# A decode block's last weight, w2: 192 of its rows laid three to a partition on 64 partitions

## The chip, the cores and the metric

The kernel runs on one core of one Trainium2 chip. The metric is device microseconds of one execution, from the first to the last thing that the core does; the median of the runs is given. Before the change it is 665.03 us, the median of three runs (664.89 to 667.58).

The core has five engines that run beside each other: PE (TensorE, matrix products, with its weight loads shown apart as PEld), DVE (VectorE), ACT (ScalarE), POOL (GpSimd) and SP (SyncE), which here only issues transfers. Sixteen DMA engines move the data.

## What is computed

One decoding step of an attention block with cache, followed by a dense block with the mish activation; four sequences, one new token each.

```python
def _A_ref(x, k_cache, v_cache, wq, wo):
    q = (x @ wq).reshape(B, Sq, H, Dh) transposed to (B, H, Sq, Dh)
    scores = jnp.einsum("bhqd,bhkd->bhqk", q, k_cache) * (Dh ** -0.5)
    p = _softmax(scores, axis=-1)
    o = jnp.einsum("bhqk,bhkd->bhqd", p, v_cache)
    return o (heads joined) @ wo

def _B_ref(x, w1, b1, w2):
    h = jnp.einsum("bsd,df->bsf", x, w1) + b1
    sp = jnp.log1p(jnp.exp(-jnp.abs(h))) + jnp.where(h > 0, h, 0)
    act = h * jnp.tanh(sp)
    return jnp.einsum("bsf,fd->bsd", act, w2)

h = x + _A_ref(_layernorm(x), k_cache, v_cache, wq, wo)
h2 = h + _B_ref(_layernorm(h), w1, b1, w2)
```

B = 4, Sq = 1, D = 640, 32 heads of 128, 4096 cached positions, F = 1728; everything is bf16. The two caches are 268 MB of the 283 MB that the kernel reads. w2 is 1728 x 640, 2.21 MB.

## The kernel before

**An order written out by hand.** A small class, `Program`, takes every operation with its engine, the things it reads and writes, and a function that emits it. `add` (L41) notes what an operation has to wait for: writers of what it reads, readers and writers of what it overwrites, and whatever is named in `after`. Each engine then runs its operations strictly in the order in which they were added, and waits on semaphores. Operations that carry a `sem` are transfers; each completed transfer adds 16 to its semaphore. SP's and POOL's operations are emitted first, as straight lists (L218); DVE, ACT and PE have a part ahead of a loop, the loop's body, and a part behind it.

**The stream.** The 16 units (8 heads of one sequence each) need one K tile and one V tile each, 128 partitions of 65,536 bytes. They go through three buffers, `slot0` to `slot2`. K is multiplied by the query on DVE (L639), summed over the head's dimensions by products with an identity on PE (L651), reduced (L626), and turned into weights of the softmax (L688 to L736); V is multiplied on PE (L761). SP issues all these transfers on one queue. As soon as a slot has been read for the last time, the weights of the end go into it: wo and w1 into slot `i1` (`wend`), w2 into slot `i2` (`wend2`), and the working tiles of the end behind w2 (`scratch`, L918).

**The order of SP's last transfers** (L884 to L914): wo in two pieces (L885), w1 in three (L886), then w2. The first w2 transfer waits for `last_pv`, the PE products that read V of the last unit but one from slot `i2`.

**How w2's rows lie.** F = 1728 is 13 blocks of 128 rows and 64 rows more. The first 12 blocks are laid in pairs: a partition takes two neighbouring rows, 2560 bytes, in one packet. Block 12 is single, 1280 bytes a partition. The pieces are `W2P = (0, 6, 10, 12, C2)`, four transfers. The 64 rows left are a transfer of their own, ahead of these: they go to every second partition (`w2r_sb[1::2, :]`, L903), over a memset to zero by POOL (L897) that they wait for.

**How the activations follow that.** `f_rows(c)` (L533) says which 128 columns of w1 block `c` takes, so that the activation comes out on the partition where its row of w2 lies: every second column for a block of a pair, 128 neighbouring ones for block 12. The block that holds the 64 left over, number `C2` = 13, takes the last 128 columns, half of which block 12 has too. `FC` = 14 blocks, so b1 is turned in 14 columns (L570), each of the five passes over w1 (`h1_pass`, L1051) makes 14 products, and the mish chain works on 56 columns (L1083 to L1113). To bring the last 64 activations to every second partition, with zeros between, a 0/1 matrix `apart` is built by POOL (L935, L938), and one PE product (L1154) and an ACT copy (L1158) move block 13's activations into `act_r`.

**The last products.** `residual` puts h into the output bank. `w2_products` (L1135) makes four products for each block, one for each quarter of the output's 640 columns. The order on PE is: residual, the turning product, blocks 0 to 5, the 64 rows left over, blocks 6 to 9, blocks 10 and 11, block 12; each piece waits for its own transfer. Then DVE and ACT gather the four quarters (L1166) and SP stores them (L1175).

Of the kernel before, what the change touches and what calls it, by code (L numbers as in the profile page):

```python
# [8 lines left out]
BF16 = mybir.dt.bfloat16  # L9
ACT = mybir.ActivationFunctionType  # L10
# [224 lines left out]
def kernel(  # L235
# [13 lines left out]
    nc = tc.nc  # L249

    B, Sq, D = A_x.shape
    _, H, Sk, Dh = A_k_cache.shape
    F = B_w1.shape[1]
    N = B * Sq
    DC = D // 128
# [20 lines left out]
    CT = 128 // (G * RQ)  # L276
    VQ = 2

    C2 = F // 128
    FM = C2 * 128  # L280
    FREM = F - FM
    FC = C2 + 1
    W2P = (0, 6, 10, 12, C2)
    W1P = (0, 2, 4, DC)
    OT4 = 4
    DT = D // OT4
    OVER = 128 - FREM


    pad = -int(nc.sbuf_base) % 512  # L290
# [11 lines left out]
    slot = [slots.tile([128, SLOT], BF16, name=f"slot{i}") for i in range(NS)]  # L302
    banks = [ps.tile([128, 512], FP32, name=f"bank{i}") for i in range(8)]
    s_bank, tr_bank, qq_bank, o_bank, oT_bank = banks[0:4], *banks[4:8]
    S_BANK, TR, QQ, OB, OT = [("bank", i) for i in range(4)], *[("bank", i) for i in range(4, 8)]

    def const(shape, dt, name):
        return consts.tile(shape, dt, name=name)

    ident = const([128, 128], BF16, "ident")  # L310
# [4 lines left out]
    nscale = const([1, 128], FP32, "nscale")  # L315
    b1T = const([128, FC], FP32, "b1T")

# [28 lines left out]
    P = Program(nc, tc, 1, NU - 1, NS)  # L346
# [4 lines left out]
    def cells(i, lo=0, hi=SLOT):  # L351

        return [("slot", i, p, k) for p in range(lo // PART, -(-hi // PART)) for k in range(NQ)]
# [5 lines left out]
    def load_kv(what, rows, u, i, parts=1):  # L359
        w = SLOT // parts  # L360
        for k in range(parts):
# [24 lines left out]
        w=cells(0, 0, o0),  # L386
        sem="wq",
# [4 lines left out]
        w=["b1"],  # L392
        sem="b1",
# [9 lines left out]
            out=ident[:, :],  # L403
            in_=ident[:, :],
# [7 lines left out]
        w=["ident"],  # L412
# [5 lines left out]
        w=["ident_f"],  # L418
# [12 lines left out]
    def bn_stats():  # L431
        for s in range(2):
# [8 lines left out]
        w=["mv"],  # L441
# [4 lines left out]
            out=ln_std[:, :], in_=ln_mv[:, 1:2], func=ACT.Sqrt, bias=eps_t[0:N, :], scale=1.0  # L446
        ),
        r=["mv", "eps"],
        w=["std"],
# [5 lines left out]
        w=["rstd1"],  # L455
# [4 lines left out]
            out=ln1_bf,  # L460
# [7 lines left out]
        w=["ln1"],  # L468
# [19 lines left out]
    for src, dst, r, w in (  # L488
# [8 lines left out]
            w=[w],  # L497
# [3 lines left out]
    def identity_sums(dst, pattern, name, **kw):  # L501
# [13 lines left out]
            out=own[:, :], in0=own1[:, :], scalar1=-1.0, scalar2=1e30, op0=ALU.add, op1=ALU.mult  # L515
        ),
        r=["own1"],
        w=["own"],
# [8 lines left out]
        w=["dq_m"],  # L527
# [3 lines left out]
    )  # L531

    def f_rows(c):  # L533
        if c < C2 - C2 % 2:
            f0 = c // 2 * 256 + c % 2
            return slice(f0, f0 + 255, 2)
        f0 = c * 128 if c < C2 else F - 128
        return slice(f0, f0 + 128)


    qT_ps = qq_bank[:, 0 : N * H].rearrange("p (b h) -> p b h", b=N)
# [1 line left out]
    def q_all():  # L543
        for h in range(H):
# [15 lines left out]
            out=qT[:, 0 : NU * G].rearrange("p (o b g) -> p b o g", o=NO, b=N),  # L560
            in_=qT_ps[:, :, :].rearrange("p b (o g) -> p b o g", o=NO),
        ),
        r=[QQ],
        w=["qT"],
    )
    b_ps = oT_bank[:, 0:FC]

    def b1_turned():
        for c in range(FC):
            ins = nc.tensor.matmul(  # L570
                b_ps[:, c : c + 1],
                lhsT=b1_row[:, f_rows(c)],
                rhs=ident[0:1, 0:1],
                start=True,
                stop=True,
            )
        return ins
# [256 lines left out]
    def slot_of(u):  # L834
        return 1 if u == 0 else 2 * u % NS

    for u in range(NU):
# [10 lines left out]
        if u >= 1:  # L848
            last_pv = pv(u - 1, 0 if u == 1 else slot_of(u - 1), u)
# [7 lines left out]
    i1, i2, i3 = slot_of(NU - 1), slot_of(NU - 2), slot_of(NU - 3)  # L857
    wend, wend2 = slot[i1], slot[i2]
# [3 lines left out]
    wo_view = A_wo.rearrange("(w p j) n -> p w j n", w=NW, j=J)  # L862
    nw2 = FC * D
    w2_sb = wend2[:, 0 : C2 * D].rearrange("p (k n) -> p k n", k=C2)
    w2r_sb = wend2[:, C2 * D : nw2]
    C2E = C2 - C2 % 2
    w2_view = B_w2[0 : C2E * 128, :].rearrange("(m p k) n -> p m (k n)", p=128, k=2)

    def load(out_ap, in_ap, i, lo, hi, name, sem=None):


        ops = {}
        for cell in cells(i, lo, hi):
            for d in P.readers.get(cell, {}).values():
                ops[d.nth] = d
        P.add(
            "SP",
            lambda: nc.sync.dma_start(out=out_ap, in_=in_ap),  # L878
            w=[name],
            sem=sem or "_".join(map(str, name)),  # L880
            after=ops.values(),
        )
# [3 lines left out]
    for k0, k1 in zip(W1P, W1P[1:]):  # L886
# [5 lines left out]
            nwo + k1 * F,  # L892
            ("w1", k0),
        )
    P.add(
        "POOL",
        lambda: nc.gpsimd.memset(w2r_sb, 0.0),  # L897
        w=["w2r"],
        after=[last_pv],
    )  # L900
    P.add(
        "SP",
        lambda: nc.sync.dma_start(out=w2r_sb[1::2, :], in_=B_w2[FM:F, :]),  # L903
        w=["w2r"],
        sem=f"slot{i2}",
    )
    for k0, k1 in zip(W2P, W2P[1:]):
        if k0 < C2E:
            assert k0 % 2 == k1 % 2 == 0
            to = wend2[:, k0 * D : k1 * D].rearrange("p (m n) -> p m n", n=2 * D)  # L910
            of = w2_view[:, k0 // 2 : k1 // 2]
        else:
            to, of = w2_sb[:, k0, :], B_w2[k0 * 128 : k1 * 128, :]
        load(to, of, i2, k0 * D, k1 * D, ("w2", k0))  # L914

    at = [nw2]
# [1 line left out]
    def scratch(n, dt=FP32):  # L918
        a = at[0]
        w = n * (2 if dt == FP32 else 1)  # L920
        w += w % 2
        at[0] = a + w
        ap = wend2[:, a : a + w]
        return ap.bitcast(FP32)[:, 0:n] if dt == FP32 else ap[:, 0:n]

    def do(eng, emit, r=(), w=()):

        return P.add(eng, emit, r=r, w=w, after=[last_pv])

    def tt(out_, a, b, op, r, w):  # L930
        do("DVE", lambda: nc.vector.tensor_tensor(out=out_, in0=a, in1=b, op=op), r, w)


    apart = scratch(128, BF16)
    do("POOL", lambda: nc.gpsimd.memset(apart, 0.0), w=["apart"])  # L935
    do(
        "POOL",
        lambda: nc.gpsimd.tensor_copy(out=apart[:, 1::2], in_=ident[:, OVER:128]),  # L938
        ["ident", "apart"],
        ["apart"],  # L940
    )


    yT = s_bank[0][:, 0 : DC * N].rearrange("p (c n) -> p c n", c=DC)
# [72 lines left out]
    def cols(n=DC, dt=FP32):  # L1017
        return scratch(n * N, dt).rearrange("p (c n) -> p c n", c=n)
# [28 lines left out]

    h1_ps = qq_bank[:, 0 : FC * N].rearrange("p (c n) -> p c n", c=FC)
    std, rstd = scratch(N), scratch(N)

    def h1_pass(dc):  # L1051
        for c in range(FC):
            ins = nc.tensor.matmul(
                h1_ps[:, c, :],
                lhsT=w1_sb[:, dc, f_rows(c)],
                rhs=h2T[:, dc, :],
                start=(dc == 0 and c == 0),
                stop=(dc == DC - 1 and c == C2),
            )
        return ins  # L1060

    for dc in range(DC):
        w1 = ("w1", max(k0 for k0 in W1P if k0 <= dc))
        do("PE", lambda dc=dc: h1_pass(dc), [w1, "h2T"], [QQ])
        if dc == 1:
            v_ps = column_means(sq, "sq")
            do(
                "ACT",
                lambda: nc.scalar.activation(
                    out=std, in_=v_ps, func=ACT.Sqrt, bias=eps_t[:, :], scale=1.0  # L1070
                ),
                [OT, "eps"],
                ["std2"],
            )
            do(
                "ACT",
                lambda: nc.scalar.activation(out=dummy[:, :], in_=eps_t[0:N, :], func=ACT.Exp),
                ["eps"],
                ["dummy"],
            )  # L1080
            do("DVE", lambda: nc.vector.reciprocal(out=rstd, in_=std), ["std2"], ["rstd"])

    h1n, h1s, ta, tb, tc_, td = (cols(FC) for _ in range(6))  # L1083
    act_t = cols(FC, BF16)
# [8 lines left out]
    def stt(out_, a, scalar, b, op0, op1, r, w):  # L1093
# [13 lines left out]
            out=tc_, in0=tb, scalar1=-0.5, scalar2=-1.0, op0=ALU.mult, op1=ALU.add  # L1107
# [26 lines left out]

    def w2_products(blocks):  # L1135
        for c in blocks:
            w2, h = (w2_sb[:, c, :], act_t[:, c, :]) if c < C2 else (w2r_sb, act_r)
            for t in range(OT4):
                ins = nc.tensor.matmul(
                    y2[32 * t : 32 * t + N, :],  # L1140
                    lhsT=h,
                    rhs=w2[:, t * DT : (t + 1) * DT],
                    start=False,
                    stop=(c == C2 - 1),
                )
        return ins

    do("PE", residual, ["hT", "ident_f"], [S_BANK[1]])

    act_r = scratch(N, BF16)  # L1150
    r_ps = oT_bank[:, 0:N]
    do(
        "PE",
        lambda: nc.tensor.matmul(r_ps, lhsT=apart, rhs=act_t[:, C2, :], start=True, stop=True),  # L1154
        ["apart", "act"],
        [OT],
    )
    do("ACT", lambda: nc.scalar.copy(out=act_r, in_=r_ps), [OT], ["act_r"])  # L1158
    for k0, k1 in zip(W2P, W2P[1:]):
        do("PE", lambda b=range(k0, k1): w2_products(b), [("w2", k0), "act"], [S_BANK[1]])  # L1160
        if k0 == 0:
            do("PE", lambda: w2_products([C2]), ["w2r", "act_r"], [S_BANK[1]])
    out_bf = scratch(D, BF16)[0:N, :]

    def gather(t, copy):
# [4 lines left out]
    for t in range(OT4):  # L1170
# [6 lines left out]
        sem="out",  # L1177
# [43 lines left out]
```

## Time and profile before

| what | value |
|---|---|
| median of three runs | 665.03 us (664.89 to 667.58) |
| the profiled execution | 665.04 us, of which the span of instructions is 663.3 us |
| granted TensorE clock, mean | 0.817 |
| DMA | 283.52 MB, mean 427 GB/s; 6685 packets |
| packets under 512 B, under 2 KB, under 8 KB | 713, 913, 2066 |
| PE busy, DVE busy | 381.9 us (58%), 352.4 us (53%) |
| ACT busy, POOL busy | 89.2 us (13%), 2.8 us |
| longest chain of waits by engine | DMA 45%, DVE 25%, PE 19% |

The span is cut into 40 slices of 16.6 us on the page; a digit is the busy share of a slice in tenths. A packet is one contiguous run of bytes that one DMA engine moves, and a transfer's completions, 4 bytes each, are counted among the packets too. In the stretches of the end, the busy share of the DMA engines and what they moved:

| us from the span's start | DMA share | GB/s | TensorE clock |
|---|---|---|---|
| 640 to 645 | 1.02 | 434 | 0.50 |
| 645 to 650 | 0.94 | 393 | 0.50 |
| 650 to 655 | 1.02 | 397 | 0.50 |
| 655 to 660 | 0.70 | 259 | 0.50 |

In the lines of the profile, "a <- b" behind an instruction names what it writes and reads; "[idle before <- releaser]" is how long its engine had waited and for whom.

### The profile page before, as it was taken

Reading aid. Unit: us, or ns where it says so; the run is one execution under the profiler, and the core shown is the slowest. Engines: PE = TensorE matmul, PEld = TensorE weight load, DVE = VectorE, ACT = ScalarE, POOL = GpSimd, SP = SyncE. Lnnn points to the kernel's source line nnn. Section 1 sums busy time; section 2 is a strip of 40 time slices with the busy share of each in tenths; the row PEclk is TensorE's granted clock in tenths of the full one; section 3 lists DMA queues with packets and bytes.
Section 4 is the critical chain, followed back from the end, with each engine's and each line's share of the span. In section 5 each row is a group of like instructions: output and inputs, shape, how many; then the busy total and the mean of one; then the engine's idle time right before and its main releaser. Section 6 shows DMA issues by size and latency. Waiting matters only on the chain.

```text
span 663.3 us, 6916 instructions
## 1 busy us (share of the span) xinstructions
PE 381.9 (58%) x2804; PEld 174.1 (26%) x2804; DVE 352.4 (53%) x313; ACT 89.2 (13%) x319; POOL 2.8 (0%) x14
## 2 busy tenths in 40 slices
PE   0254868375481837548183754818375481837675
PEld 0221323132230313223031322303132230313344
DVE  2075868184573818457381845738184573818502
ACT  0102020202002020200202020020202002020211
POOL 1000000000000000000000000000000000000000
PEclk9998888879695987969598796959879695987955
DMA  9999999999999999999999999999999999999997
GB/s 380 444 439 440 439 417 419 444 431 436 435 435 431 427 443 423 443 435 431 431 431 439 427 443 435 427 431 435 439 427 439 431 431 427 443 427 439 417 421 275
DMA packets 6685, 283.52 MB, mean 427 GB/s; under 512 B 713, under 2 KB 913, under 8 KB 2066
## 3 DMA queue, kind: packets, MB, share of 16 engines
q1 hardware_dynamic: 6664, 283.35, 99.1%
q8 instruction: 8, 0.13, 0.1%
q10 hardware_dynamic: 10, 0.01, 0.0%
q14 instruction: 3, 0.02, 0.0%
HBM read 283.35 MB, written 0.01 MB: 427 GB/s over the span
## 4 chain that ended last, share of the span: by engine, by line
DMA 45%; DVE 25%; PE 19%; another core or an unknown queue 6%; issue 2%; SPq 2%; ACT 1%; DVEq 0%; POOL 0%; ACTq 0%
DMA slot<-in_A_k_cache_dram 41%; DVE slot L639 21%; PE bank L651 13%; PE bank L761 5%; DMA slot<-in_B_w_dram 3%; DVE s_sb L626 3%; SPq L878 2%; ACT e L736 1%; PE bank L719 0%; DVE mx L706 0%; DVE rl L813 0%; PE bank L697 0%; DVE otn L820 0%; DVEq L228 0%
## 5 line engine op out<-in xcount | busy, mean ns | idle before, releaser
L651 PE MATMUL bank<-slot,ident 128*128 128x512 bf16 x1024 | 274.4, 423 | 242.8 <-DVE slot L639 242.8
L639 DVE TENSOR_TENSOR slot<-slot,qb 128x4096 bf16<-128x4096 bf16 x128 | 288.3, 2284 | 153.0 <-DMA slot<-in_A_k_cache_dram 148.6
L651 PEld LDWEIGHTS bank<-slot,ident 128*128 128x128 bf16 x1024 | 101.4, 107 | 401.0 <-DVE slot L639 275.2
L626 DVE TENSOR_REDUCE s_sb<-bank 128x64 f32<-128x512 f32 x64 | 44.0, 688 | 59.1 <-PE bank L651 59.1
L736 ACT ACTIVATE e<-s_sb,nb 128x256 bf16<-128x256 f32 x128 | 63.1, 495 | 45.6 <-DVE nb L728 45.6
L761 PE MATMUL bank<-slot,e 128*32 128x512 bf16 x1024 | 61.8, 395 | 4.4 <-DMA slot<-in_A_v_cache_dram 2.6
L606 ACT CAST qb<-bank 128x128 bf16<-128x128 f32 x17 | 4.5, 266 | 307.4 <-PE bank L597 307.4
L761 PEld LDWEIGHTS bank<-slot,e 128*32 128x32 bf16 x1024 | 26.3, 99 | 37.9 <-issue 9.6
L781 ACT COPY o_sb<-bank 128x512 f32<-128x512 f32 x16 | 9.4, 586 | 183.4 <-PE bank L761 183.4
L706 DVE TENSOR_REDUCE mx<-bank 1x8 f32<-1x128 f32 x16 | 4.5, 278 | 39.9 <-PE bank L697 39.9
L736 ACT ACTIVATION_READ_ACCUMULATOR e<-s_sb,nb 128x1 f32 x128 | 23.9, 187 | 0.0
L794 PE MATMUL bank<-sel,o_sb 128*128 128x8 f32 x136 | 18.5, 262 | 0.0
L794 PEld LDWEIGHTS bank<-sel,o_sb 128*128 128x128 f32 x136 | 17.4, 200 | 0.0
L813 DVE RECIPROCAL rl<-bank 128x8 f32<-128x8 f32 x17 | 3.4, 202 | 15.3 <-PE bank L794 15.3
L546 PE MATMUL bank<-xT,slot 128*128 128x4 bf16 x160 | 4.4, 168 | 10.5 <-DMA slot<-in_A_wq_dram 10.5
L719 PE MATMUL bank<-mx,nscale 1*128 1x8 f32 x32 | 6.1, 262 | 5.9 <-DVE mx L706 5.9
L580 DVE COPY b1T<-bank 128x14 f32<-128x14 f32 x1 | 0.2, 172 | 13.8 <-PE bank L570 13.8
L792 PEld LDWEIGHTS bank<-rs,ones_f 128*128 128x128 f32 x34 | 6.5, 197 | 3.8 <-ACT o_sb L781 1.6
L719 PEld LDWEIGHTS bank<-mx,nscale 1*128 1x128 f32 x32 | 4.7, 182 | 10.6 <-DVE mx L706 10.6
L546 PEld LDWEIGHTS bank<-xT,slot 128*128 128x128 bf16 x160 | 4.3, 104 | 10.5 <-DMA slot<-in_A_wq_dram 10.5
L688 DVE TENSOR_REDUCE pm<-s_sb 128x1 f32<-128x256 f32 x16 | 6.7, 420 | 0.5
L697 PE MATMUL bank<-ident_f,pm 128*1 128x128 f32 x32 | 6.1, 272 | 1.2 <-DVE pm L688 1.2
(80 smaller groups left out, 68.2 us busy)
## 6 DMA issues: line engine op xcount, KB each, us to landing
slot<-in_A_v_cache_dram SPq DMA_DIRECT2D x2, 4096.0 KB, 44.5
slot<-in_A_wq_dram SPq DMA_DIRECT2D x1, 5120.0 KB, 15.2
slot<-in_A_wo_dram SPq DMA_DIRECT2D x2, 2560.0 KB, 32.7
slot<-in_B_w_dram SPq DMA_DIRECT2D x2, 864.0 KB, 33.1
slot<-in_B_w_dram SPq DMA_DIRECT2D x1, 960.0 KB, 30.4
slot<-in_B_w_dram SPq DMA_DIRECT2D x1, 640.0 KB, 31.9
slot<-in_B_w_dram SPq DMA_DIRECT2D x1, 432.0 KB, 32.2
slot<-in_B_w_dram SPq DMA_DIRECT2D x1, 320.0 KB, 22.2
```

What stands on the lines that cost most here:

```text
L546: ins = nc.tensor.matmul(qT_ps[:, :, h], lhsT=wq_sb[:, c, h * Dh : (h + 1) * Dh], rhs=xT[:, c, :], start=(c == 0), stop=(c == DC - 1),)
L626: lambda: nc.vector.tensor_reduce(out=s_sb[:, part * RP : (part + 1) * RP], in_=s_bank[part][:, :].rearrange("p (r w) -> p r w", w=W), axi ...
L639: return nc.vector.tensor_tensor(out=kt, in0=kt, in1=qbs[u % NS][:, k * DQ : (k + 1) * DQ] .unsqueeze(1) .to_broadcast([128, RP, DQ]), op= ...
L651: ins = nc.tensor.matmul(s_bank[part][:, :].rearrange("p (r w) -> p r w", w=W), lhsT=ident[:, :], rhs=kt[:, :, d : d + W], start=(d == 0), ...
L688: lambda: nc.vector.tensor_reduce(out=pm[:, :], in_=s_sb[:, :], axis=AX.X, op=ALU.max),
L719: lambda: nc.tensor.matmul(nb_ps, lhsT=nscale[:, :], rhs=mx[:, :], start=True, stop=True),
L736: ins = nc.scalar.activation(out=e2[:, :, h, :], in_=s_sb[:, :].rearrange("p (g r) -> p g r", r=RQ), func=ACT.Exp, bias=nb[:, h : h + 1], ...
L761: ins = nc.tensor.matmul(o_bank[t : t + G * RQ, :], lhsT=e2[:, g, :, :], rhs=vt[:, g * RQ : (g + 1) * RQ, :], start=(g < CT), stop=(g >= N ...
L781: lambda: nc.scalar.copy(out=o_sb[:, :], in_=o_bank[:, :]),
L792: nc.tensor.matmul(l_ps, lhsT=ones_f[:, :], rhs=rss[u % NS][:, :], start=True, stop=True)
L794: ins = nc.tensor.matmul(o_ps, lhsT=o_sb[:, r * Dh : (r + 1) * Dh], rhs=sel[:, r, :], start=(r == 0), stop=(r == RQ - 1),)
L878: lambda: nc.sync.dma_start(out=out_ap, in_=in_ap),
```

## The change

w2 is divided the other way round. Its first 192 rows (`FR`) come first: `PR` = 64 partitions take `KR` = 3 neighbouring rows each, 3840 bytes, and no partition is left empty between them. They are issued as eight transfers of eight rows, transfer `p` with partitions p, p + 8, ..., p + 56. All eight count on one semaphore. Behind them follow `C2` = 12 blocks of 128 rows: ten in pairs and two single, in the pieces (0, 6, 10, 11, 12).

POOL's memset of the remainder, the matrix `apart`, the turning product and the ACT copy are gone. The 192 rows are three blocks of 64 partitions in `w2_products`; their activations come from `f_rows`, which takes every third of 382 columns of w1 for them (the lower 64 partitions are used). `FC` is 15 for 14. In the order on PE, the three blocks come right behind the residual, ahead of block 0, and wait for all eight transfers.

```diff
-    C2 = F // 128
-    FM = C2 * 128
-    FREM = F - FM
-    FC = C2 + 1
-    W2P = (0, 6, 10, 12, C2)
+    C2 = F // 128 - 1
+    PR = 64
+    KR = (F - C2 * 128) // PR
+    FR = PR * KR
+    FC = C2 + KR
+    C2E = C2 - 2
+    W2P = (0, 6, C2E, C2 - 1, C2)
...
     def f_rows(c):
-        if c < C2 - C2 % 2:
-            f0 = c // 2 * 256 + c % 2
+        if c < C2E:
+            f0 = FR + c // 2 * 256 + c % 2
             return slice(f0, f0 + 255, 2)
-        f0 = c * 128 if c < C2 else F - 128
-        return slice(f0, f0 + 128)
+        if c < C2:
+            return slice(FR + c * 128, FR + (c + 1) * 128)
+
+        return slice(c - C2, c - C2 + 127 * KR + 1, KR)
...
-    w2r_sb = wend2[:, C2 * D : nw2]
+    w2r_sb = wend2[0:PR, C2 * D : nw2]
...
-    P.add(
-        "POOL",
-        lambda: nc.gpsimd.memset(w2r_sb, 0.0),
-        w=["w2r"],
-        after=[last_pv],
-    )
-    P.add(
-        "SP",
-        lambda: nc.sync.dma_start(out=w2r_sb[1::2, :], in_=B_w2[FM:F, :]),
-        w=["w2r"],
-        sem=f"slot{i2}",
-    )
+    for p in range(8):
+        load(
+            w2r_sb[p::8, :],
+            B_w2[0:FR, :].rearrange("(p s) n -> p (s n)", s=KR)[p::8, :],
+            i2,
+            C2 * D,
+            nw2,
+            ("w2r", p),
+            f"slot{i2}",
+        )
...
-    apart = scratch(128, BF16)
-    do("POOL", lambda: nc.gpsimd.memset(apart, 0.0), w=["apart"])
-    do(
-        "POOL",
-        lambda: nc.gpsimd.tensor_copy(out=apart[:, 1::2], in_=ident[:, OVER:128]),
...
     def w2_products(blocks):
         for c in blocks:
-            w2, h = (w2_sb[:, c, :], act_t[:, c, :]) if c < C2 else (w2r_sb, act_r)
+            if c < C2:
+                w2, h = w2_sb[:, c, :], act_t[:, c, :]
+            else:
+                w2, h = w2r_sb[:, (c - C2) * D : (c - C2 + 1) * D], act_t[0:PR, c, :]
...
-    act_r = scratch(N, BF16)
-    r_ps = oT_bank[:, 0:N]
     do(
         "PE",
-        lambda: nc.tensor.matmul(r_ps, lhsT=apart, rhs=act_t[:, C2, :], start=True, stop=True),
-        ["apart", "act"],
-        [OT],
-    )
-    do("ACT", lambda: nc.scalar.copy(out=act_r, in_=r_ps), [OT], ["act_r"])
+        lambda: w2_products(range(C2, FC)),
+        [*[("w2r", p) for p in range(8)], "act"],
+        [S_BANK[1]],
+    )
     for k0, k1 in zip(W2P, W2P[1:]):
         do("PE", lambda b=range(k0, k1): w2_products(b), [("w2", k0), "act"], [S_BANK[1]])
-        if k0 == 0:
-            do("PE", lambda: w2_products([C2]), ["w2r", "act_r"], [S_BANK[1]])
```

More of the change, by code (lines that the diff above doesn't have):

```diff
@@ L277 @@
     VQ = 2
-    C2 = F // 128
-    FM = C2 * 128
-    FREM = F - FM
-    FC = C2 + 1
-    W2P = (0, 6, 10, 12, C2)
+    C2 = F // 128 - 1
+    PR = 64
+    KR = (F - C2 * 128) // PR
+    FR = PR * KR
+    assert FR + C2 * 128 == F
+    FC = C2 + KR
+    C2E = C2 - 2
+    W2P = (0, 6, C2E, C2 - 1, C2)
     W1P = (0, 2, 4, DC)
@@ L286 @@
     DT = D // OT4
-    OVER = 128 - FREM
     pad = -int(nc.sbuf_base) % 512
@@ L864 @@
     w2_sb = wend2[:, 0 : C2 * D].rearrange("p (k n) -> p k n", k=C2)
-    w2r_sb = wend2[:, C2 * D : nw2]
-    C2E = C2 - C2 % 2
-    w2_view = B_w2[0 : C2E * 128, :].rearrange("(m p k) n -> p m (k n)", p=128, k=2)
+    w2r_sb = wend2[0:PR, C2 * D : nw2]
+    w2_view = B_w2[FR : FR + C2E * 128, :].rearrange("(m p k) n -> p m (k n)", p=128, k=2)
     def load(out_ap, in_ap, i, lo, hi, name, sem=None):
@@ L912 @@
         else:
-            to, of = w2_sb[:, k0, :], B_w2[k0 * 128 : k1 * 128, :]
+            to, of = w2_sb[:, k0, :], B_w2[FR + k0 * 128 : FR + k1 * 128, :]
         load(to, of, i2, k0 * D, k1 * D, ("w2", k0))
@@ L931, in tt @@
         do("DVE", lambda: nc.vector.tensor_tensor(out=out_, in0=a, in1=b, op=op), r, w)
-    apart = scratch(128, BF16)
-    do("POOL", lambda: nc.gpsimd.memset(apart, 0.0), w=["apart"])
-    do(
-        "POOL",
-        lambda: nc.gpsimd.tensor_copy(out=apart[:, 1::2], in_=ident[:, OVER:128]),
-        ["ident", "apart"],
-        ["apart"],
-    )
     yT = s_bank[0][:, 0 : DC * N].rearrange("p (c n) -> p c n", c=DC)
@@ L1057, in h1_pass @@
                 start=(dc == 0 and c == 0),
-                stop=(dc == DC - 1 and c == C2),
+                stop=(dc == DC - 1 and c == FC - 1),
             )
```

## The prediction

> **What bounds the kernel now.** I read the strip of 40 slices first, then the queue table, the chain of waits of the last part, the order in time around the w2 issues, and the two groups of instructions that the change makes longer. From the page:
>
> ```profile
> DMA  9999999999999999999999999999999999999997
> ...
> q1 hardware_dynamic: 6664, 283.35, 99.1%
> q8 instruction: 8, 0.13, 0.1%
> q10 hardware_dynamic: 10, 0.01, 0.0%
> ```
>
> The 16 DMA engines are full in every slice but the last, so the kernel ends when the bytes are through; the change moves none of them away (w2 is 1728 x 640 x 2 = 2.21 MB before and after). Only the last microseconds can move. The chain of waits there:
>
> ```profile
> 637.23 22.25 DMA slot<-in_B_w_dram
> 659.48 0.04 issue
> 659.52 0.74 PE bank L1139 x9
> 660.26 0.02 issue
> 660.29 0.31 DVE slot L1166
> 660.60 0.01 issue
> 660.62 0.32 DVE slot L1166
> ```
>
> From the last w2 byte to the end lie 0.74 us of products (nine, the last four behind the last piece), 0.65 us of gathers and the store. None of that is edited, so what counts is when the last w2 piece lands. In order of time, the issues and the operations that go:
>
> ```profile
> 624.93 0.63 POOL L897 MEMSET slot<- 128x640 bf16 x1 [621.55 <-PE bank L761]
> 625.50 0.20 POOL L935 MEMSET slot<- 128x128 bf16 x1
> 625.59 0.55 SPq L903 DMA_DIRECT2D slot<-in_B_w_dram  x1
> 625.77 0.26 POOL L938 COPY slot<-ident 128x64 bf16<-128x64 bf16 x1
> 626.18 21.97 SPq L878 DMA_DIRECT2D slot<-in_B_w_dram  x4
> ```
>
> The trace's packet records give the first 2560-byte packet of w2 at 651.8 us and the first of w2's remainder at 651.6: 26 us behind their issues, because V's last half, wo and w1 stand ahead on each engine. The median packet takes 0.055 us for 1280 bytes, 0.106 for 2560, 0.135 for 3456 and 0.266 for 6912, and an engine's completion mark follows its data at once: the 16 completions of the old remainder (four packets an engine) came 0.21 us behind those of the piece before. So an engine's end is the sum of its packets.
>
> **The last landing.** The 16 engines end apart. The completions of the last piece run from 657.64 to 659.89 us: eight before 658.73, seven from 659.22 to 659.50, one at 659.89. The late ones are those that had to carry an instruction fetch (the eight q8 packets, 16 KB, about 1 us each; the last starts at 656.5, and one engine's completion moves from ninth to last across it).
>
> **Change, transfers.** Per engine, w2 is now 48 packets of 2560, 8 of 1280 and 4 of 1280 for the remainder: 48 x 0.106 + 12 x 0.055 = 5.75 us. After, the pairs are ten blocks (40 x 0.106 = 4.24) and two single blocks follow (16 x 0.055 = 0.88): 5.12 us on every engine. The 64 rows of 3840 bytes come on top; between 0.135 and 0.266 us by size a packet is 0.150. How many engines share them is not shown for eight rows. The nearest rows: q10's ten packets are x (four rows) and b1 (one row), so 4 + 1 data packets and 4 + 1 completions, one engine a row; transfers of 64 and 128 rows have 16 completions. Bounds: all sixteen (4 x 0.150 = 0.60, sum 5.72, -0.03 us) and one engine for all 64 rows (9.6, sum 14.7, +9.0 us). I take eight, one row each, as x's four went to four, and the same eight for every transfer, because b1's one packet ran on an engine that also carried a row of x. These eight then have 8 x 0.150 + 5.12 = 6.32 us, **+0.57**, and the other eight 5.12, **-0.63**.
>
> [...]
>
> The end is the latest engine's. It gains only if all seven late engines and the straggler are among the unburdened. With one of the seven burdened it moves to 659.50 + 0.57 = 660.07 (+0.18); with the straggler burdened, to 660.46 (+0.57). I can't tell the late engines' numbers, and that not one of seven is among eight of sixteen is unlikely by count, so I take the middle, **+0.4 us**, bounds -0.63 and +0.57.
>
> **Change, POOL and SP.** Gone: 0.63 + 0.20 + 0.26 us of POOL and its wait in front of SP, so the first remainder issue can go at 624.9 where pv ends, not 625.59. Added: seven issues, at 0.33 to 0.58 us each as the neighbours took, 2.3 to 4.1 us, all ahead of the four w2 issues. The first w2 piece is then issued at about 628 to 629.5 for packets due at 651.8: nothing, covered by over 22 us of queue. SP's later issues are held up by a full queue (10.4, 9.1 and 1.4 us), the last until 648.15; its packets run from about 658. Eleven more entries on a burdened engine (16 instead of 5) delay it by eleven w1 packets, 11 x 0.266 = 2.9 us, to 651: still covered by 6 us. Only the store is behind on SP. Should that cover go, each microsecond late is one on the end.
>
> **Change, PE and the vector engines.**
>
> ```profile
> L1139 PE MATMUL bank<-slot 128*4 128x160 bf16 x56 | 2.5, 326 | 0.6 <-DMA slot<-in_B_w_dram 0.5
> L1053 PEld LDWEIGHTS bank<-slot,slot 128*128 128x128 bf16 x70 | 2.2, 107 | 0.4 <-issue 0.4
> L1053 PE MATMUL bank<-slot,slot 128*128 128x4 bf16 x70 | 2.1, 166 | 0.4 <-DVE slot L931 0.4
> L1154 PE MATMUL bank<-slot 128*128 128x4 bf16 x1 | 0.2, 164 | 1.3 <-issue 1.3
> ```
>
> Fifteen blocks for fourteen: five more h1 products (2.15 us / 70 = 0.031 each, +0.15), four more w2 products (28 in 1.10 us, 0.039 each, +0.16), four more columns on 56 in six DVE and ACT operations (0.22 us each, so under 0.1 together), one more b1 product at 20 us where DVE then waits 13.8 us. The turning product (0.16) goes; the ACT copy behind it ran beside w2 products. The remainder's products now stand first: activations at 656.94 + 0.25 = 657.2, then 36 products, 1.4 us, to 658.6. The second w2 piece landed at 658.70 and PE sat 0.5 us for it: hidden there, and the last four products still start behind the last landing. The remainder itself lands by 653.93 + 1.2 = 655.1, before 657.2. Stride-3 weight columns are not in the trace; strides of one and two both load at 0.104 us. Taken: the same. Upper bound, twice: 15 x 0.104 = 1.6 us before the activations, PE done with 60 products (2.35 us) at 661.15 where it is now done at 660.26: +0.9 us.
>
> **Sum.** 0 (POOL, SP) + 0 (PE, hidden) + 0.4 (landing): span 663.3 + 0.4 = 663.7. The profiled execution took 665.04, 1.74 more than its span, and the median is 665.03, so **665.4 us**, no change. What can be told from no change is 0.5%, 3.3 us; the three runs lie 2.7 us apart.
>
> **Rivals.**
> (a) The burdened engines are the early eight. For it: the late and early halves are nearly eight and eight. Against: engines carry fetches for reasons that have nothing to do with rows. -0.63: 664.4.
> (b) Two engines get in each other's way. [...] Eight rows then cost 2.4, not 1.2 us, on a burdened engine: +0.57 + 1.2 = 1.8, 666.8 us. For it: x's first packets, with other traffic starting, took up to 0.40 us instead of 0.053. Against: 0.21 us for the old remainder's four packets, though its rows stepped over partitions too. [...]
> (c) Slower: the queue counts transfers, not entries. When SP first stuck (626.8), eight were outstanding, and it came free at 637.2, after V landed (636.4). Were eight the limit, the third remainder transfer would wait for V, the next for wo and w1, and w2 would be issued only when w1 is through at 653.9. From wq's issue to its first packet took 1.0 us, a held issue up to another; four late issues cost 0.5 each: a dry queue of 2 to 4 us, 667.4 to 669.4, from the point where the first w2 issue passes 651. Against: the next two releases, 646.4 and 648.15, fall on no landing (642.5, 648.6), as entries would have it.
> (d) The eight rows stay on fewer engines: on two, 32 x 0.150 + 5.12 - 5.75 = +4.2, 669.2; on one, 674.0. Against: x's four packets on four engines.
> (e) Faster by over 0.5%: nothing offers 3.3 us; if all engines ended together the gain would be about 1.
>
> **Chances.** Forecast 0.52, (a) 0.17, (b) 0.14, (c) 0.09, (d) 0.05, (e) 0.03. Slower by over 0.5% (past 668.4) is half of (c), nearly all of (d), and what lies beyond (b): 0.10; faster 0.03; within 0.87. The range holds the forecast, (a), (b) and the start of (c): 664.2 to 667.4, which takes in the weight loads' +0.9 and the middle of the three runs' spread.
>
> **What would show it.** After: q1 with 6712 packets (64 completions for 16, data unchanged at 960), so 761 under 512 B, 1025 under 2 KB, 2114 under 8 KB; with sixteen engines per transfer it would be more. No POOL work after 620 us. SP's eight issues from 624.9, the w2 issues behind, the last ending by about 651; if past 655, (c). The remainder landed by 655 to 656; past 656.5, (b). The last w2 completions split into two groups 1.2 us further apart or closer than now. Span over 667 would make the forecast wrong.

## The result, and the profile after

The changed kernel takes 668.18 us (median of ten runs, 666.98 to 669.34); the kernel before, 665.02 us in the ten runs beside them. The ratio is 1.0037, interval 1.0026 to 1.0047: slower by 0.37%, clear of the noise, though within the 0.5% that the prediction had named as its bound for no change. The forecast time was 665.4 us and its range 664.2 to 667.4, so the median lies above the range.

The profiled execution is one of 668.18 us, with a span of 666.3 us. The page's counts:

```profile
DMA packets 6733, 283.52 MB, mean 426 GB/s; under 512 B 761, under 2 KB 1025, under 8 KB 2114
## 3 DMA queue, kind: packets, MB, share of 16 engines
q1 hardware_dynamic: 6712, 283.35, 99.0%
```

All four packet counts are those of the forecast for eight engines a transfer (6712; 761, 1025, 2114): 48 packets more on q1, 64 completions for the old remainder's 16. So the transfers went out in eights as assumed, and what was mispriced is what the packets do. The stretches of the end show it; first the kernel before, then the changed one (columns: stretch, its length, busy time of PE, PEld, DVE, ACT and POOL with counts, TensorE clock, DMA share, GB/s):

```profile
650.00:655.00 5.00, 4.16 (x118) 4.00 (x116) 1.30 (x8) 1.23 (x2) 0.00 (x0) 0.50 1.02 397
655.00:660.00 5.00, 3.14 (x79) 1.81 (x73) 1.43 (x6) 0.82 (x4) 0.00 (x0) 0.50 0.70 259
```

```profile
650.00:655.00 5.00, 2.93 (x84) 2.79 (x85) 0.69 (x5) 0.00 (x0) 0.00 (x0) 0.50 1.03 354
655.00:660.00 5.00, 3.78 (x99) 3.24 (x99) 1.50 (x8) 2.00 (x4) 0.00 (x0) 0.50 1.00 312
660.00:665.00 5.00, 2.44 (x60) 1.43 (x60) 1.22 (x4) 0.57 (x2) 0.00 (x0) 0.50 0.20 72
```

The DMA share in 650 to 655 us is the same, 1.02 and 1.03, but the bytes are not: 397 and 354 GB/s. The engines are as busy and move less: here a busy share of 1.03 came with 354 GB/s.

The chain of waits, from the stretch in which w1's last piece lands:

```profile
621.90 36.01 DMA slot<-in_B_w_dram
657.91 0.05 issue
657.96 0.57 PE bank L1045 x15
...
660.40 0.23 DVE slot L1088
660.63 0.14 issue
660.76 2.13 PE bank L1134 x53
662.90 0.03 issue
662.93 0.33 PE bank L1134 x4
```

In this execution even w1 came late: its last piece landed at 657.91 us, where it was 653.93 before. Not all of that comes from the new packets. The latest engine was 2.55 us behind already when wo's last piece landed (651.18 us, before 648.63), and the first new packet started only at 652.52 us. Behind w1 come the activations and all 60 products of w2, almost without a gap in the chain, and the last of w2 landed at 662.88, as those products ended. Transfers and PE reach the end together here.

**A measure for it.** The trace has the duration of every packet. The sum, over w1's and w2's packets after 640 us, of what each took above the ordinary time of its size (0.055 us for 1280 bytes, 0.106 for 2560, 0.135 for 3456, 0.149 for 3840, 0.266 for 6912) is called the lost engine time below. Sixteen engines share it, so 16 us lost delay the whole stream by about 1 us.

```
kernel        lost engine time, us   of it 3840 B   2560 B   3456 B   median 3840 B packet
before                2.3                -            0.8      0.2         -
changed              26.3               5.5          15.0      2.8       0.236 us
```

The 64 new packets do take 0.236 us for 0.149, but that is a fifth of it. Most of the loss lies on packets that were not changed at all: w2's 2560-byte ones and the end of w1.

**All engines are slowed together.** The two profiles between 654 and 656 us, first before, then changed:

```profile
654.00:656.00 2.00, 1.77 (x54) 1.40 (x50) 0.88 (x5) 1.64 (x4) 0.00 (x0) 0.50 1.04 397
```

```profile
654.00:656.00 2.00, 1.63 (x34) 1.58 (x34) 0.63 (x4) 0.00 (x0) 0.00 (x0) 0.50 1.03 233
```

In the changed kernel, 194 packets of w1 and w2 start between 654.0 and 656.5 us, and 156 of them are unchanged ones. Not one of these 156 took its ordinary time: the least slowed took 1.21 times as long, the median one 1.67 times. In the kernel before, no packet of that stretch took more than 1.08 times its ordinary time. The last new packet ended at 656.79 us, and from 657.5 to 658.5 us the median is back at 1.00. So, while the new packets are under way, the unchanged packets are slowed as much (1.67 times at the median) as the new ones (0.236 us for 0.149, 1.58 times).

### The profile page after: what moved, and what is told of

Same layout as the page of the kernel before. It is cut to its first block, busy times and chain, and to the rows that moved or that the text cites. A ratio compares the mean times of both kernels' runs of the same rounds, so it can differ in the third digit from the quotient of the medians.

```text
span 666.3 us, 6936 instructions
## 1 busy us (share of the span) xinstructions
PE 378.0 (57%) x2813; PEld 173.5 (26%) x2813; DVE 352.5 (53%) x313; ACT 89.1 (13%) x318; POOL 1.8 (0%) x11
## 2 busy tenths in 40 slices
DMA packets 6733, 283.52 MB, mean 426 GB/s; under 512 B 761, under 2 KB 1025, under 8 KB 2114
## 3 DMA queue, kind: packets, MB, share of 16 engines
q1 hardware_dynamic: 6712, 283.35, 99.0%
## 4 chain that ended last, share of the span: by engine, by line
DMA 46%; DVE 25%; PE 18%; another core or an unknown queue 6%; issue 2%; ACT 1%; DVEq 0%; SPq 0%; ACTq 0%
DMA slot<-in_A_k_cache_dram 41%; DVE slot L643 21%; PE bank L655 13%; DMA slot<-in_B_w_dram 5%; PE bank L765 5%; DVE s_sb L630 3%; ACT e L740 1%; PE bank L1134 0%; PE bank L723 0%; DVE mx L710 0%; DVE rl L817 0%; PE bank L701 0%; DVE otn L824 0%; DVEq L228 0%
## 5 line engine op out<-in xcount | busy, mean ns | idle before, releaser
L655 PE MATMUL bank<-slot,ident 128*128 128x512 bf16 x1024 | 270.2, 418 | 247.3 <-DVE slot L643 247.3
```

Source lines behind the costliest of these rows:

```text
L655: ins = nc.tensor.matmul(s_bank[part][:, :].rearrange("p (r w) -> p r w", w=W), lhsT=ident[:, :], rhs=kt[:, :, d : d + W], start=(d == 0), ...
```

## The experiments

Two theories stood: **P**, the packets are slowed by where their rows are written, engines getting in each other's way (the prediction's rival (b), with a price several times higher), and **F**, the profiled execution only had its instruction fetches on engines that were late already. A price of eight transfers as such, or of the uneven load, was a third. Lost engine time is from the one profiled execution of each kernel; "before" beside each time is the kernel before, on the same chip.

**The change once more.**

> The changed kernel once more, for a second profile. [...] Theory F (the profiled run was late because instruction fetches fell on engines that were already late, and the transfers only add 0.6 us of uneven load): the packets' times repeat, but w1's last landing is within 1.5 us of 653.9 us in this profile. Time by both 667 to 669 us.

667.40 us (before 665.22), ratio 1.0034, interval 1.0017 to 1.0051. 28.7 us of engine time lost, median of the new packets 0.198 us (0.236 in the first profile), w1's last landing at 657.88. The loss repeats. The late landing of w1 does not tell P from F, since 2.3 us of it were there already when wo's last piece landed (650.90 us, in the kernel before 648.63). An engine late beforehand, as F has it, does occur: this profile, of a 670.19 us run, had one engine 2.1 us behind the next latest when V of the last unit but one landed (619.22 and 617.08 us), long before the changed transfers. That instruction fetches made it late is not shown.

**Rows four partitions apart in place of eight.**

```diff
     for p in range(8):
+        q0 = p // 4 * 32 + p % 4
+        rows = slice(q0, q0 + 29, 4)
         load(
-            w2r_sb[p::8, :],
-            B_w2[0:FR, :].rearrange("(p s) n -> p (s n)", s=KR)[p::8, :],
+            w2r_sb[rows, :],
+            B_w2[0:FR, :].rearrange("(p s) n -> p (s n)", s=KR)[rows, :],
```

> [...] Theory P: 3840-byte packets at 0.15 us, w1's last landing back at about 654 us plus the skew of the run, time 665.2 to 666.2 us, 2 us or more under the change. Theory F, or a price of the eight transfers as such (issue, completion marks, uneven load): as the change, 667.5 to 669 us, packets still at 0.23 us or so.

665.31 us (before 665.22), ratio 0.9999, interval 0.9990 to 1.0009. Every one of the 64 packets took 0.149 us, the longest too; 2.0 us of engine time lost; w1 landed at 653.94. The whole loss of the change is gone, with the same count of transfers, the same bytes, the same packet counts (so again in eights) and the same number of issues on SP. The stretch 650 to 655 us of this kernel:

```profile
650.00:655.00 5.00, 4.15 (x119) 3.99 (x118) 1.18 (x7) 1.15 (x2) 0.00 (x0) 0.50 1.00 400
```

400 GB/s at a share of 1.00, as before the change. PE's order in time in this kernel also answers the prediction's step on the products:

```profile
657.24 1.47 PE L1136 MATMUL bank<-slot 64*4 64x160 bf16 x36 [1.31 <-DVE slot L1090]
659.29 1.18 PE L1136 MATMUL bank<-slot 128*4 128x160 bf16 x24 [0.59 <-DMA slot<-in_B_w_dram]
```

The first 36 products start at 657.24 and take 1.47 us (forecast 657.2 and 1.4), and PE then waits 0.59 us for a transfer: hidden, as costed.

**Eight neighbouring partitions, and one transfer of 64.** The rows are `slice(8 * p, 8 * p + 8)` in the one, the whole of `w2r_sb` in the other.

> [...] Theory P: a packet takes 0.4 to 0.6 us, eight of them 3.2 to 4.8 us on the burdened engines instead of 1.9: time 669.5 to 671.5 us. Theory F or a price per transfer: as the change, 667.5 to 669 us.

> [...] Theory P: packets at 0.2 to 0.3 us, but four instead of eight on an engine: 665.5 to 667 us. A price per transfer or of the uneven load alone: 665.0 us, as the kernel before, packets at 0.15 us. Theory F: within 0.5 us of the change.

Neighbours: 667.27 us, ratio 1.0034 (1.0020 to 1.0049), 21.4 us lost, 0.204 us a packet. The expectation was 669.5 us or more, from an estimate of 0.4 to 0.6 us a packet: a miss. One transfer: 667.15 us, ratio 1.0030 (1.0019 to 1.0042), 28.0 us lost, 0.251 us a packet; up to 667 was expected. It rules out a price per transfer, and uneven load as the cause: one transfer of 64 rows costs as much as eight transfers of eight (667.15 and 667.40 us). Its time is within 0.5 us of the change, as F had it too, but F is out by the kernel with rows four apart. And eight neighbouring partitions to a transfer cost no more than rows eight apart (21.4 us lost for 28.7).

**Half the dose.** Partitions 0 to 31 come by four transfers of rows four apart, partitions 32 to 63 by four transfers of eight neighbouring partitions.

```diff
+        rows = slice(p, p + 29, 4) if p < 4 else slice(8 * p, 8 * p + 8)
```

> [...]

666.47 us (before 665.30), ratio 1.0018 (1.0008 to 1.0027): 1.17 us, a little over half of the 2.05 us that the neighbours cost. The profile, from a 669.98 us run, lost 17.3 us, more than half of the neighbours' 21.4; one engine was over 2 us behind in it (V's landing at 620.0). So in time it is not all or nothing. That the loss grows with the bytes written to neighbouring partitions rests on this one comparison. The single transfer of 64 rows wrote the same bytes to the same partitions as the neighbours' eight, and it lost 28.0 us; what sets the size of the loss stays open.

**By itself, on the kernel before.** Eight more transfers into a place that nothing uses, ahead of w2's pieces, in the two shapes. Nothing else of the change is in these kernels.

```diff
+    spare = wend2[0:64, 24576 : 24576 + 3 * D]
+    for p in range(8):
+        rows = slice(p, p + 57, 8)
+        load(
+            spare[rows, :],
+            B_w2[0:192, :].rearrange("(p s) n -> p (s n)", s=3)[rows, :],
...
```

> The kernel before, with eight more transfers of eight rows of 3840 bytes into a place that nothing uses, ahead of the w2 pieces, rows four partitions apart (nothing else is changed; 0.25 MB more are read, and the output is the same). [...] If the end is set by one of the burdened engines, as the prediction's +0.57 had it: 666.2 to 666.5 us. If the late engines are among the other eight: 665.0 to 665.4 us. 3840-byte packets at 0.149 us in both.

> The same extra transfers on the kernel before, but rows eight partitions apart as in the change. Theory P: 2 us or so over the one with rows four apart, 667.5 to 668.8 us, with 2560-byte packets of w2 slowed as well. Rival (the loss needs something else of the change: three rows taken three apart by PE, the new order of products, no POOL work): equal to the one with rows four apart within 0.5 us.

Four apart: 666.16 us (before 665.30), ratio 1.0015 (1.0003 to 1.0028), 1.7 us lost. Eight apart: 667.98 us, ratio 1.0035 (1.0021 to 1.0049), 34.7 us lost, packets at 0.259 us. 1.8 us between them, where the bytes and the count of transfers are equal: it needs nothing else of the change. The 0.9 us of the first is between what uneven load (8 x 0.149 = 1.2, if all eight transfers ran on the same eight engines, which no view shows) and the bytes spread out (0.25 MB at 427 GB/s, 0.6) would give.

**Which side, and which partitions.** The shape of the rows read and of the partitions written was changed one at a time; then the four-apart rows were written to partitions 64 to 127 (`spare = wend2[64:128, ...]`).

> Which side of the transfer it is. The kernel before with the eight extra transfers, written to partitions four apart, but read from rows of w2 eight apart (the spare bytes are used by nothing). If the place written decides (theory P): as with four apart on both sides, 665.9 to 666.4 us, no 3840-byte packet over 0.16 us, under 3 us of engine time lost. If the place read in memory decides: 667.5 us or more, packets at 0.2 us and over.

> The other half: read four rows apart, written eight partitions apart. Theory P: 667.5 to 668.6 us, 25 to 35 us of engine time lost. If the place read decides: 665.9 to 666.4 us.

> [...] If two engines of one transfer have to meet (pairs): as on partitions 0 to 63, 665.9 to 666.4 us. If it is enough to write where another engine writes in the pieces around (owner): 667.5 us or more, with 2560-byte packets slowed most.

Read eight apart, written four apart: 665.86 us (before 665.08), ratio 1.0018 (1.0009 to 1.0027), 1.6 us lost. Read four, written eight apart: 668.13 us, ratio 1.0051 (1.0036 to 1.0067), 30.5 us lost. The place written decides (2.3 us between the two); the place read does nothing that can be seen.

On the upper 64 partitions: 669.15 us, ratio 1.0060 (1.0043 to 1.0078), the dearest of all, with 40.7 us lost and packets at 0.279 us. The same step of four lost 1.7 us on partitions 0 to 63. So the step between the rows of a transfer does not decide alone, and the forecast that held is the owner's. As an explanation it stays the author's estimate: which engine writes where no view shows, nor does any run tell whether the others have to be writing there at that moment. The upper partitions as such are not the cause: the next kernel writes half its rows to partitions 64 to 95 and loses 2.0 us, the kernel before 2.3. The stretches of the two kernels, four apart on partitions 0 to 63 and then on 64 to 127:

```profile
650.00:655.00 5.00, 4.15 (x123) 4.01 (x120) 1.17 (x7) 0.89 (x2) 0.00 (x0) 0.50 1.01 402
655.00:660.00 5.00, 2.63 (x70) 1.86 (x71) 1.57 (x6) 1.17 (x4) 0.00 (x0) 0.50 0.82 308
```

```profile
650.00:655.00 5.00, 4.15 (x117) 4.01 (x118) 0.99 (x6) 0.00 (x0) 0.00 (x0) 0.50 1.02 336
655.00:660.00 5.00, 2.40 (x65) 1.89 (x63) 1.74 (x7) 2.16 (x5) 0.00 (x0) 0.50 1.05 283
```

Again equal shares, 1.01 and 1.02, at 402 and 336 GB/s. And again all engines are slowed together: of the 263 unchanged packets that start between 653.5 and 657.5 us in the second kernel, the least slowed took 1.36 times its ordinary time; of the 585 in the first, none took over 1.08 times.

**Partitions 32 to 95.** The 192 rows go there, by four transfers of 16 rows four apart.

```diff
-    w2r_sb = wend2[0:PR, C2 * D : nw2]
+    w2r_sb = wend2[32 : 32 + PR, C2 * D : nw2]
...
+    for p in range(4):
+        load(
+            w2r_sb[p::4, :],
+            B_w2[128 : 128 + FR, :].rearrange("(p s) n -> p (s n)", s=KR)[p::4, :],
```

> [...] (The rows are 128 to 319 here, the single blocks are the last and the first 128 rows; POOL zeroes the other 64 partitions, and the products run over all 128.) Theory P: no packet slowed, 5.72 us for w2 on every engine as in the kernel before, 664.9 to 665.4 us. [...] Rival (packets of 3840 bytes or 64 partitions cost as such): 666.5 us or more.

665.23 us (before 665.30), ratio 1.0001 (0.9989 to 1.0013), 2.0 us lost, packets at 0.149 us, the last landing at 659.85 (659.89 before). Three rows to a packet and 64 partitions cost nothing in this placement, and gain nothing either. Each measured against the kernel before on its own chip, this kernel (-0.07 us) and the one with eight transfers four apart (+0.09) lie 0.16 us apart, inside both intervals: the uneven load can't be told from nothing.

**Why the old remainder was not slowed.** The kernel before, with one extra transfer of 64 rows of 3840 bytes to every second partition, `spare[1::2, :]` of 128.

> The kernel before with 64 extra rows of 3840 bytes in one transfer to every second partition of 128, the placement that its own remainder has. Its 1280-byte packets there were not slowed (0.055 us). If that placement keeps each of the sixteen engines where it writes in the pieces around (theory P, owner form): 3840-byte packets at 0.149 us, under 3 us of engine time lost, the bytes alone spread over sixteen engines, +0.6 us: 665.5 to 666.0 us. If it was only too short to be seen: 20 us or more of engine time lost and 667 us or more, as one transfer to 64 neighbouring partitions.

Packets at 0.151 us, the longest 0.161, 2.5 us lost: this placement does not slow the longer packets either, so the old remainder was not merely too short. The time, 666.39 us (before 664.98), ratio 1.0016 (1.0007 to 1.0024), is 0.4 us over what was expected; the profiled run's latest engine was at 618.11 us at V's landing, 1.2 us behind the one of the profile before. That lateness was there ahead of the transfers; whether it explains the median too is not shown.

## Why the prediction was wrong

- **Eight engines a transfer, the same eight:** the packet counts are exact for eight a transfer (64 completions). By number the engines are not shown, nor whether they are the same eight each time.
- **3840 bytes at 0.150 us:** right for an undisturbed packet (0.149), wrong for these (0.236).
- **The landing, +0.4 us, is the term that failed.** Engines in each other's way were taken at nothing and left to rival (b), chance 0.14, priced at 1.2 us on the burdened engines alone, 666.8 in all. No run shows (b)'s doubling, 2.4 us for 1.2: the new packets took 0.236 us for 0.149, 1.58 times. They were slowed, as (b) had it, but (b) was too small: it priced the new packets alone, which lost 5.5 us, where the unchanged packets beside them were slowed too. The unchanged 2560-byte packets lost 15.0 us. All in all it is 24 us more engine time than before, 1.5 us for each of sixteen. In this execution the last landing moved by 3.0 us, but the latest engine stood 2.55 us later already at wo's last piece, ahead of the new packets. Averaged over the engines, the last piece landed 2.4 us later (661.22 us, before 658.85), and 1.0 us of that was there at wo's last piece (648.77, before 647.72); the 1.3 left fits the 1.5. So the price of the change is read from the medians, 3.2 and 2.2 us in the two sets of runs, against 0.1 for rows four apart, and not from this one landing.
- **The prediction's own sign of (b)** held: the last of the 64 rows landed at 657.85 us, past the 656.5 that it had named, and at 655.58 us with rows four apart.
- **The evidence that was read against (b) was read wrongly.** The old remainder's four packets at 0.21 us were taken to show that stepping over partitions costs nothing. They showed one placement, every second of 128, which the last run found to disturb nothing with 3840-byte packets either (0.151 us a packet, 2.5 us lost).
- **Two engines in each other's way,** (b)'s condition, is not shown. By placement, the extra transfers lost 34.7 us with rows eight apart, 1.7 with rows four apart on partitions 0 to 63, and 40.7 with rows four apart on 64 to 127. Eight neighbouring partitions to a transfer (21.4 us lost, 0.204 us a packet) lost no more than rows eight apart, and no run shows the 0.4 to 0.6 us a packet estimated for them. Nor is the loss confined to the new packets, since between 654.0 and 656.5 us no unchanged packet escaped it. Why such a transfer slows the packets beside it, no run shows.
- **Uneven load, +0.57 and -0.63:** not shown. Two kernels that lost nothing, one uneven by the prediction's count and one even, lie at 665.31 and 665.23 us, both equal to the kernel before within their intervals. So (a)'s gain of 0.63 does not show either.
- **SP and POOL at nothing:** right. The issues took 0.56 to 0.73 us each, more than the 0.33 to 0.58 costed, the last w2 issue ended at 651.7 (forecast 651), and the kernel with rows four apart has the same issues and loses nothing. One issue of the changed kernel lasted 19.20 us (10.37 the longest before); that a full queue holds an issue up is the author's reading. So rival (c) is out; and (d) by the counts.
- **PE and the vector engines at nothing:** right where transfers are not slowed. Weight columns three apart load in 0.104 us, as taken.

Two things stay open: through what such placements slow the packets of all transfers under way, and why an execution's latest engine is late before the changed part is reached. The prediction put such lateness down to instruction fetches, which no experiment moved. The times of one kernel spread over 1.4 to 4.2 us here, those of the kernel before over 1.4 to 2.9.

## What to carry to other kernels

Where small transfers between large ones write is to be chosen by measurement. In this kernel eight rows four partitions apart on the lower 64 partitions, sixteen such rows on partitions 32 to 95, or every second partition of 128 in one transfer disturbed nothing (1.7 to 2.5 us of engine time lost, 2.3 in the kernel before); rows eight apart, 64 neighbouring partitions in one transfer or in eight, and rows four apart on the upper 64 did (21.4 to 40.7 us). Price a transfer that disturbs by all the packets that are under way beside it, not by its own: of the 26.3 us lost, 5.5 lay on the new packets. And read the DMA share together with the GB/s: here 1.03 at 354 GB/s, where it had been 1.02 at 397, was the sign.

## What was not expected of the hardware

0.25 MB in 64 packets, 0.09% of the kernel's bytes, made the kernel about 3 us longer on partitions 64 to 127 than on 0 to 63 (669.15 and 666.16 us). The 40.7 us of engine time lost there are four times the 64 x 0.149 = 9.5 us that the packets themselves need, because the packets beside them are slowed while they are under way (each of 263, by 1.36 times or more), and the engines look fully busy meanwhile (a share of 1.02 at 336 GB/s).
